# Keys and values of a decode attention kernel in tiles of four heads and 32 KB rows, where they were in tiles of two heads and 16 KB rows

## The chip, the cores and the metric

The kernel runs on one core of one Trainium2 chip. Its metric is the time on the device in microseconds (us), the median of several executions; lower is better. "Span" is the time from the first to the last instruction that the profiler saw in one execution; it is 1.7 to 2.1 us shorter than the time of the same execution. All runs compared here were in the fast state; e1 and e2, single looks below, have no state of their own (unknown), and lie within 0.3% of the fast runs beside them.

## The reference, cut to what matters

One token goes through an attention with 32 heads over a window of 4096 cached keys and values, times a gate from a small feed-forward block.

```python
# Hq = Hkv = 32 heads, Dh = 128, W = 4096 (the end of a cache of 32768), D = 512
q = (xn @ wq).reshape(B, 1, Hq, Dh).transpose(0, 2, 1, 3)
k = k_cache[:, :, Sk - W:, :]
v = v_cache[:, :, Sk - W:, :]
scores = einsum("bhqd,bhkd->bhqk", q, k) * Dh ** -0.5
o = einsum("bhqk,bhkd->bhqd", softmax(scores), v)
s = o.transpose(0, 2, 1, 3).reshape(B, 1, Hq * Dh) @ wo
# [the feed-forward block that gives g is cut: its weights are 4 % of the bytes]
return x + s * silu(g)
```

All is bfloat16. Keys and values are 67.1 MB of the 78.84 MB that the kernel reads, and each byte is used once.

## The kernel before

A step takes the keys of two heads. Each head fills every other partition, so a partition's row is 64 keys of 128 numbers, 16 KB in one piece of memory. VectorE computes a part of the scores itself (`k_vector`: a multiplication and a sum, two pieces to a step). TensorE turns the rest of the keys, ScalarE copies them out, and TensorE multiplies them with the query (`k_turn`, `k_scores`). The softmax goes by groups of four heads, so two steps; the values follow three steps behind the keys. All loads go through one queue, in the program's order.

```python
G, LAG, K_BUFS, V_BUFS = 4, 3, 6, 3
def load_kv(pool, cache, i, cuts=None):              # two heads, 2 MB
    t = pool.tile([P, CP, Dh], BF16, tag="kv", name="kv")          # CP = 64
    src = cache[0, 2 * i:2 * i + 2, W0:, :].rearrange("a (b c) d -> b a (c d)", b=P // 2)
    ...
def k_vector(s, kn, half):
    ...
    nc.vector.tensor_tensor(out=prod[:, 0:m, :], in0=kn[:, rows, :],
                            in1=q_bc[:, s:s + 1, :].to_broadcast([P, m, Dh]), op=ALU.mult)
    nc.vector.tensor_reduce(out=st[s // 2]["S"][:, s % 2, rows], in_=prod[:, 0:m, :], axis=AX.X, op=ALU.add)
...
for s in range(NP + LAG):                            # NP = 16 steps
    h = s - LAG
    kn = load_kv(k_pool, A_k_cache, s) if s < NP else None
    ...
    elif h >= 0:
        v = load_kv(v_pool, A_v_cache, h)
    ...
        k_vector(s, kn, 0)
        k_turn(s, kn)
        for g in turn:
            sm_turn(g)                               # maximum over partitions: PE, then DVE
        if s % 2 == 1 and s >= 3:
            sm_den((s - 3) // 2)                     # PE: sum over partitions
            sm_rden((s - 3) // 2)                    # DVE: 1 / sum
        k_scores(s)
        ...                                          # own scores, exponentials
        k_vector(s, kn, 1)
        if h >= 0:
            v_pair(h, v)                             # PE: values times weights
        ...
        if s % 2 == 1:
            sm_max(s // 2)                           # DVE: maximum along the row
```

Of the kernel before, what the change touches and what calls it, by code (L numbers as in the profile page):

```python
# [8 lines left out]
P = 128  # L9
BF16 = mybir.dt.bfloat16  # L10
# [9 lines left out]
LAG = 3  # L20
K_BUFS = 6
NE = 4
V_BUFS = 3
EARLY = 4
LATE = 14
# [4 lines left out]
def kernel(  # L30
# [24 lines left out]
    CP = 2 * W // P  # L55
# [7 lines left out]
    kt_pool = ctx.enter_context(tc.tile_pool(name="kt", bufs=2))  # L63
# [9 lines left out]
    small.tile([P, 64], BF16, name="pad")  # L73
# [22 lines left out]
    def load_kv(pool, cache, i, cuts=None):  # L96
        t = pool.tile([P, CP, Dh], BF16, tag="kv", name="kv")
        src = cache[0, 2 * i:2 * i + 2, W0:, :].rearrange("a (b c) d -> b a (c d)", b=P // 2)
        dst = t[:].rearrange("p c d -> p (c d)")
        cuts = cuts or (0, CP)  # L100
        for c0, c1 in zip(cuts, cuts[1:]):
            load(dst[:, c0 * Dh:c1 * Dh], src[:, :, c0 * Dh:c1 * Dh])
            if len(cuts) > 2 and c1 == cuts[-2]:
                load_rows(H - 4, 2)
        return t
# [13 lines left out]
    sel = wts.tile([H, H // 2, P // 2, 2], BF16, name="sel")  # L119
    nc.vector.tensor_copy(out=sel[:], in_=ident_bf[0:H, 0:H].rearrange("k (i a) -> k i a", a=2).unsqueeze(2)  # L120
                          .to_broadcast([H, H // 2, P // 2, 2]))
# [125 lines left out]
    q_bc = small.tile([P, H // 2, Dh], BF16, name="q_bc")  # L247
    for i in range(0, H // 2, 4):
        qb_ps = ps_tr.tile([P, 4, Dh], FP32, tag="pt", name="qb_ps")
        for k in range(4):  # L250
            nc.tensor.matmul(qb_ps[:, k, :], lhsT=sel[:, i + k, :, :].rearrange("k b a -> k (b a)"),
                             rhs=q_rows[:], start=True, stop=True)
        nc.scalar.copy(out=q_bc[:, i:i + 4, :], in_=qb_ps[:])
# [7 lines left out]
    for c in range(2):  # L261
# [14 lines left out]
    par = const.tile([P, 2], FP32, name="par")  # L276
    nc.vector.tensor_reduce(out=par[:], in_=ident_f[:].rearrange("p (b a) -> p a b", a=2), axis=AX.X,
                            op=ALU.max)
    two = const.tile([4, 1], FP32, name="two")
    nc.vector.tensor_reduce(out=two[:], in_=ident_f[0:4, 0:2], axis=AX.X, op=ALU.max)  # L280
    par_t = const.tile([4, P // 2, 2], FP32, name="par_t")
    nc.vector.tensor_scalar(out=par_t[:], in0=ident_f[0:4, 2:4].unsqueeze(1).to_broadcast([4, P // 2, 2]),
                            scalar1=two[:], scalar2=None, op0=ALU.add)
    md = const.tile([4, 2, 2], FP32, name="md")
    nc.vector.tensor_scalar(out=md[:], in0=ident_f[0:4, 2:4].unsqueeze(1).to_broadcast([4, 2, 2]),
                            scalar1=-1.0, scalar2=1e30, op0=ALU.add, op1=ALU.mult)




    pick_f = const.tile([P, 4, 2, 2], FP32, name="pick_f")
    for r in range(2):
        nc.vector.tensor_copy(out=pick_f[:, :, r, :],
                              in_=ident_bf[:, 32 * r:32 * r + 8].rearrange("p (i a) -> p i a", a=2))
# [3 lines left out]
    def nd(s):  # L298

        return 32 if s < EARLY else 40 if s < LATE else 32  # L300

    def k_open(s):
        if s % 2 == 0:
            st[s // 2] = {
                "sT": ps_s.tile([P, 2, CP - 32, 2], FP32, tag="sT", name="sT"),
                "S": sm_pool.tile([P, 2, CP], FP32, tag="S", name="S"),
            }

    def k_vector(s, kn, half):
        m = nd(s) // 2  # L310
        rows = slice(m * half, m * half + m)
        prod = prod_pool.tile([P, 20, Dh], BF16, tag="prod", name="prod")
        nc.vector.tensor_tensor(out=prod[:, 0:m, :], in0=kn[:, rows, :],  # L313
                                in1=q_bc[:, s:s + 1, :].to_broadcast([P, m, Dh]), op=ALU.mult)
        nc.vector.tensor_reduce(out=st[s // 2]["S"][:, s % 2, rows], in_=prod[:, 0:m, :], axis=AX.X,  # L315
                                op=ALU.add)
# [3 lines left out]
    def k_turn(s, kn):  # L320
        n = nd(s)
        kts[s] = kt_pool.tile([P, CP - 32, P], BF16, tag="kt", name="kt")
        w = 8 if n % 8 == 0 else 7
        assert (CP - n) % w == 0
        for b in range(0, CP - n, w):
            pt = ps_tr.tile([P, 8, P], BF16, tag="pt", name="pt")
            for i in range(w):
                nc.tensor.transpose(pt[:, i, :], kn[:, n + b + i, :], ident_bf[:])  # L328
            nc.scalar.copy(out=kts[s][:, b:b + w, :], in_=pt[:, 0:w, :])  # L329

    def k_scores(s):
        kt = kts.pop(s)
        for c in range(CP - nd(s)):
            nc.tensor.matmul(st[s // 2]["sT"][:, s % 2, c, :], lhsT=kt[:, c, :],  # L334
                             rhs=qT_bf[:, 2 * s:2 * s + 2], start=True, stop=True)


    def sm_own(g):
        s = st[g]
        n = nd(2 * g)  # L340
        own = sm_pool.tile([P, 2, CP - 32], FP32, tag="own", bufs=1, name="own")
        nc.scalar.mul(own[:, :, 0:CP - n], s["sT"][:, :, 0:CP - n, 1], par[:, 1:2])
        s["own"] = own

    def sm_max(g):
        s = st[g]
        n = nd(2 * g)
        own = s["own"]
        nc.vector.scalar_tensor_tensor(out=s["S"][:, :, n:CP], in0=s["sT"][:, :, 0:CP - n, 0],
                                       scalar=par[:, 0:1], in1=own[:, :, 0:CP - n],  # L350
                                       op0=ALU.mult, op1=ALU.add)
        s["m1"] = sm_pool.tile([P, 2], FP32, tag="m1", name="m1")
        nc.vector.tensor_reduce(out=s["m1"][:], in_=s["S"][:], axis=AX.X, op=ALU.max)  # L353

    def sm_turn(g):

        s = st[g]
        mt_ps = ps_misc.tile([2, P], FP32, tag="misc", name="mt_ps")
        nc.tensor.transpose(mt_ps[:], s["m1"][:], ident_f[:])
        mx = sm_pool.tile([2, 2], FP32, tag="mx", name="mx")  # L360
        nc.vector.tensor_reduce(out=mx[:], in_=mt_ps[:].rearrange("r (b a) -> r a b", a=2), axis=AX.X,
                                op=ALU.max)
        nc.vector.scalar_tensor_tensor(out=md[0:2],  # L363
                                       in0=ident_f[0:2, 0:2].unsqueeze(2).to_broadcast([2, 2, 2]),
                                       scalar=-scale, in1=mx[:].unsqueeze(1).to_broadcast([2, 2, 2]),
                                       op0=ALU.mult, op1=ALU.mult)

    def sm_exp(g):
        s = st[g]
        mb_ps = ps_misc.tile([P, G], FP32, tag="misc", name="mb_ps")  # L370
        nc.tensor.matmul(mb_ps[:], lhsT=par_t[:].rearrange("k b a -> k (b a)"),  # L371
                         rhs=md[:].rearrange("k r a -> k (r a)"), start=True, stop=True)
        mb = sm_pool.tile([P, G], FP32, tag="mb", name="mb")
        nc.scalar.copy(out=mb[:], in_=mb_ps[:])  # L374
        s["pT"] = sm_pool.tile([P, 2, CP, 2], BF16, tag="pT", name="pT")
        s["sum"] = sm_pool.tile([P, G], FP32, tag="sum", name="sum")
        for i in range(G):
            nc.scalar.activation(out=s["pT"][:, i // 2, :, i % 2], in_=s["S"][:, i // 2, :], func=ACT.Exp,  # L378
                                 scale=scale, bias=mb[:, i:i + 1], accum_out=s["sum"][:, i:i + 1])

    def sm_den(g):
        s = st[g]
        s["den"] = den_ps = ps_misc.tile([P, G], FP32, tag="misc", name="den_ps")
        nc.tensor.matmul(den_ps[:], lhsT=ones_f[:], rhs=s["sum"][:], start=True, stop=True)

    def sm_rden(g):
        s = st[g]
        den_ps = s["den"]
        s["rden"] = sm_pool.tile([P, G], FP32, tag="rden", name="rden")
        nc.vector.reciprocal(out=s["rden"][:], in_=den_ps[:])  # L390
# [11 lines left out]
    def load_wo(i):  # L402
        h0, n = blocks[i]
        t = k_pool.tile([P, 16, D], BF16, tag="kv", name="wo_16")
        wo_blk[i] = t[:, 0:n, :]
# [16 lines left out]
    def v_pair(h, v, c0=0, c1=CP):  # L422
        g, r = divmod(h, 2)
        s = st[g]
        if g in MOVED:
            if r == 0:
                s["ov"] = ps_o.tile([P, 4, Dh], FP32, tag="oT", name="ov")
                nc.tensor.matmul(s["ov"][:], lhsT=zero_bf[:], rhs=v[:, 0:4, :], start=True, stop=False,
                                 skip_group_check=True)
            for c in range(0, CP, 4):  # L430
                nc.tensor.matmul(s["ov"][32 * r:32 * r + 8],  # L431
                                 lhsT=s["pT"][:, r, c:c + 4, :].rearrange("p i a -> p (i a)"),
                                 rhs=v[:, c:c + 4, :], start=False, stop=c == CP - 4,
                                 skip_group_check=True)
            if r == 1:
                s["ov_sb"] = sm_pool.tile([P, 4, Dh], FP32, tag="ov_sb", bufs=1, name="ov_sb")
                nc.scalar.copy(out=s["ov_sb"][:], in_=s["ov"][:])
        else:
            if r == 0:
                s["oT"] = ps_o.tile([P, G], FP32, tag="oT", name="oT")  # L440
            for c in range(c0, c1):
                nc.tensor.matmul(s["oT"][:, 2 * r:2 * r + 2], lhsT=v[:, c, :], rhs=s["pT"][:, r, c, :],  # L442
                                 start=(c == 0), stop=(c == CP - 1))

    def v_add(g):
        s = st[g]
        s["oT"] = ps_misc.tile([P, G], FP32, tag="misc", name="oT")
        for j in range(4):
            nc.tensor.matmul(s["oT"][:], lhsT=s["ov_sb"][:, j, :],  # L449
                             rhs=pick_f[:, j, :, :].rearrange("p r a -> p (r a)"),  # L450
                             start=(j == 0), stop=(j == 3))

    def v_out(h, n):
# [192 lines left out]
```

## Time and profile before

| before | |
|---|---|
| time, median of 3 (lowest, highest) | 195.67 us (195.56, 195.85) |
| span of the profiled execution (another one, of 196.92 us) | 195.1 us |
| key load, 2 MB: issue to landing, median | 29.9 us |
| VectorE busy, share of the span | 74% |
| share of the DMA engines taken by the load queue | 96.1% |

Two lines of the page that the prediction does not show, from its groups of instructions (busy us, mean ns of one, idle time before):

```profile
L378 ACT ACTIVATE pT<-S,mb 128x64 bf16<-128x64 f32 x32 | 10.9, 356 | 0.2
...
L462 DVE TENSOR_TENSOR o<-oT,rden 128x2 bf16<-128x2 f32 x3 | 0.5, 160 | 11.1 <-PE oT L442 11.1
```

The first is the exponential over 64 columns, which has 128 after the change. The second shows VectorE's waits in the last part of the span: 11.1 us of idle time before three tiny instructions there, all for a product of TensorE.

### The profile page before, as it was taken

How to read it: one execution, taken by the hardware profiler on the slowest of the kernel's cores; microseconds unless marked ns; L12 is line 12 of the kernel's file. 1: busy time of each engine (PE TensorE's matmuls, PEld its weight loads, DVE VectorE, ACT ScalarE, POOL GpSimd, SP SyncE). 2: the span in 40 equal slices, each digit the busy share in tenths (PEclk: the TensorE clock that was granted, in tenths of full speed). 3: DMA queues.
4: the chain of work that ended last, by engine and by line, in shares of the span. 5: the costliest groups of instructions: out<-in, count | busy, mean ns of one | idle time of the engine just before them, and what ended most of it. 6: DMA issues, size and time to landing. Idle time of an engine off the chain costs nothing.

```text
span 195.1 us, 4727 instructions
## 1 busy us (share of the span) xinstructions
PE 137.3 (70%) x2108; PEld 105.2 (54%) x2108; DVE 145.2 (74%) x164; ACT 79.0 (40%) x173; POOL 6.3 (3%) x13
## 2 busy tenths in 40 slices
PE   0549779673785899397977957367767897957751
PEld 0434469563784945235967342167656536945640
DVE  0550109999999999999999999079899996982001
ACT  2003019881945742327467053152555018933000
POOL 2110007000000000000000000000000000000000
PEclk9999966967558559759687696965555569675555
DMA  6999999999999999999999999999999999999980
GB/s 200 413 415 410 373 427 423 428 420 430 430 423 430 430 425 427 433 430 430 423 430 430 427 433 427 430 433 430 430 430 427 430 422 432 423 433 420 402 311 4
DMA packets 7052, 79.13 MB, mean 406 GB/s; under 512 B 889, under 2 KB 1753, under 8 KB 2265
## 3 DMA queue, kind: packets, MB, share of 16 engines
q1 hardware_dynamic: 6880, 78.84, 96.1%
q8 instruction: 16, 0.26, 0.5%
q10 hardware_dynamic: 152, 0.00, 0.0%
q14 instruction: 4, 0.02, 0.0%
HBM read 78.84 MB, written 0.00 MB: 404 GB/s over the span
## 4 chain that ended last, share of the span: by engine, by line
DVE 47%; DMA 24%; PE 17%; ACT 5%; issue 4%; SPq 1%; POOL 1%; POOLq 0%
DVE S L315 28%; DVE prod L313 15%; DMA kv<-in_A_v_cache_dram 15%; DMA wo_rows<-in_A_wo_dram 7%; ACT kt L329 4%; PE yr_ps L507 3%; PE oT L442 3%; PE ov L431 3%; DMA x_bf<-in_A_x_dram 2%; PE qT_ps L239 2%; PE hr_ps L223 2%; SPq L78 1%; PE a_ps L212 1%; PE hr_ps L220 1%; DVE m L353 1%
## 5 line engine op out<-in xcount | busy, mean ns | idle before, releaser
L315 DVE TENSOR_REDUCE S<-prod 128x20 f32<-128x2560 bf16 (+1 forms) x32 | 83.8, 2620 | 1.1
L329 ACT COPY kt<-pt 128x1024 bf16<-128x1024 bf16 x54 | 50.9, 1021 | 28.0 <-PE pt L328 28.0
L313 DVE TENSOR_TENSOR prod<-kv,q_bc 128x2560 bf16<-128x2560 bf16 (+1 forms) x32 | 44.3, 1385 | 9.0 <-DMA kv<-in_A_k_cache_dram 6.4
L328 PE MATMUL pt<-ident_bf,kv 128*128 128x128 bf16 x432 | 41.0, 277 | 10.4 <-DMA kv<-in_A_k_cache_dram 8.8
L328 PEld LDWEIGHTS <-kv 128*128 128x128 bf16 x432 | 37.4, 129 | 13.7 <-DMA kv<-in_A_k_cache_dram 10.2
L334 PE MATMUL sT<-qT_bf,kt 128*128 128x2 bf16 x432 | 17.7, 165 | 11.8 <-ACT kt L329 11.2
L442 PE MATMUL oT<-pT,kv 128*128 128x2 bf16 x768 | 22.3, 165 | 4.6 <-DMA kv<-in_A_v_cache_dram 4.6
L442 PEld LDWEIGHTS <-kv 128*128 128x128 bf16 x768 | 21.4, 102 | 6.0 <-DMA kv<-in_A_v_cache_dram 5.9
L334 PEld LDWEIGHTS <-kt 128*128 128x128 bf16 x432 | 15.9, 102 | 14.8 <-ACT kt L329 14.0
L431 PE MATMUL ov<-kv,pT 128*8 128x512 bf16 x64 | 21.9, 517 | 0.0
L431 PEld LDWEIGHTS <-pT 128*8 128x8 bf16 x64 | 6.7, 109 | 13.9 <-issue 11.4
L378 ACT ACTIVATE pT<-S,mb 128x64 bf16<-128x64 f32 x32 | 10.9, 356 | 0.2
L371 PE MATMUL mb_ps<-md,par_t 4*128 4x4 f32 x16 | 3.9, 314 | 9.5 <-DVE md L363 9.5
L374 ACT COPY mb<-mb_ps 128x4 f32<-128x4 f32 x8 | 1.3, 162 | 19.3 <-PE mb_ps L371 19.3
L371 PEld LDWEIGHTS mb_ps<-md,par_t 4*128 4x128 f32 x16 | 3.4, 263 | 10.1 <-issue 8.8
L462 DVE TENSOR_TENSOR o<-oT,rden 128x2 bf16<-128x2 f32 x3 | 0.5, 160 | 11.1 <-PE oT L442 11.1
L466 ACT ACTIVATE o<-oT,rden 128x1 bf16<-128x1 f32 x26 | 4.7, 264 | 6.6 <-PE oT L449 4.7
L226 DVE COPY hr<-hr_ps 1x512 f32<-1x512 f32 x1 | 0.7, 677 | 7.9 <-PE hr_ps L223 7.9
L507 PE MATMUL yr_ps<-wo,ox 128*1 128x512 bf16 x16 | 6.3, 576 | 0.0
L378 ACT ACTIVATION_READ_ACCUMULATOR pT<-S,mb 128x1 f32 x32 | 6.0, 187 | 0.0
L157 PE MATMUL ln_ps<-x_f,ones_f 128*128 128x4 f32 x4 | 1.2, 364 | 6.1 <-DVE x_f L180 5.1
L215 ACT ACTIVATE a_bf<-a_ps 128x10 bf16<-128x10 f32 x1 | 0.2, 180 | 12.4 <-PE a_ps L212 12.4
(116 smaller groups left out, 95.1 us busy)
## 6 DMA issues: line engine op xcount, KB each, us to landing
kv<-in_A_k_cache_dram SPq DMA_DIRECT2D x16, 2048.0 KB, 29.9
kv<-in_A_v_cache_dram SPq DMA_DIRECT2D x15, 2048.0 KB, 26.9
wq_sb<-in_A_wq_dram SPq DMA_DIRECT2D x1, 4096.0 KB, 19.1
wo<-in_A_wo_dram SPq DMA_DIRECT2D x1, 2048.0 KB, 28.2
w_sb<-in_B_w_dram SPq DMA_DIRECT2D x1, 1376.0 KB, 6.7
w_sb<-in_B_w_dram SPq DMA_DIRECT2D x1, 1024.0 KB
wo<-in_A_wo_dram SPq DMA_DIRECT2D x1, 1024.0 KB, 26.8
kv<-in_A_v_cache_dram SPq DMA_DIRECT2D x1, 1024.0 KB
```

Of the source, the lines that this page charges most:

```text
L223: nc.tensor.matmul(hr_ps[:], lhsT=a_bf[0:m, i:i + 1], rhs=w4_sb[0:m, i, :], start=False, stop=(i == len(chunks) - 1))
L313: nc.vector.tensor_tensor(out=prod[:, 0:m, :], in0=kn[:, rows, :], in1=q_bc[:, s:s + 1, :].to_broadcast([P, m, Dh]), op=ALU.mult)
L315: nc.vector.tensor_reduce(out=st[s // 2]["S"][:, s % 2, rows], in_=prod[:, 0:m, :], axis=AX.X, op=ALU.add)
L328: nc.tensor.transpose(pt[:, i, :], kn[:, n + b + i, :], ident_bf[:])
L329: nc.scalar.copy(out=kts[s][:, b:b + w, :], in_=pt[:, 0:w, :])
L334: nc.tensor.matmul(st[s // 2]["sT"][:, s % 2, c, :], lhsT=kt[:, c, :], rhs=qT_bf[:, 2 * s:2 * s + 2], start=True, stop=True)
L371: nc.tensor.matmul(mb_ps[:], lhsT=par_t[:].rearrange("k b a -> k (b a)"), rhs=md[:].rearrange("k r a -> k (r a)"), start=True, stop=True)
L378: nc.scalar.activation(out=s["pT"][:, i // 2, :, i % 2], in_=s["S"][:, i // 2, :], func=ACT.Exp, scale=scale, bias=mb[:, i:i + 1], accum_o ...
L431: nc.tensor.matmul(s["ov"][32 * r:32 * r + 8], lhsT=s["pT"][:, r, c:c + 4, :].rearrange("p i a -> p (i a)"), rhs=v[:, c:c + 4, :], start=F ...
L442: nc.tensor.matmul(s["oT"][:, 2 * r:2 * r + 2], lhsT=v[:, c, :], rhs=s["pT"][:, r, c, :], start=(c == 0), stop=(c == CP - 1))
L466: nc.scalar.mul(o_blk[b][:, c + k:c + k + 1], st[g]["oT"][:, hl + k:hl + k + 1], st[g]["rden"][:, hl + k:hl + k + 1])
L507: nc.tensor.matmul(yr_ps[:], lhsT=ox_blk[i][:, t:t + 1], rhs=wo_blk[i][:, t, :], start=(t == 0), stop=(t == n - 1))
```

## The change

Its intent is to have fewer and larger transfers: a tile takes four heads, interleaved over the partitions, so a row is 32 KB and a load 4 MB. The group of the softmax becomes the group of a tile, which makes some of the mask work simpler. The key buffers hold as many bytes as before in half as many pieces (3 of 32 KB to a partition, where it was 6 of 16); the value buffers hold a third more in fewer pieces (2 of 32 KB, where it was 3 of 16). Cut to its core:

```diff
-LAG = 3
-K_BUFS = 6
+LAG = 2
+K_BUFS = 3
-V_BUFS = 3
+V_BUFS = 2
-    CP = 2 * W // P
+    CP = G * W // P                                   # 128 columns of 128 numbers
-    def load_kv(pool, cache, i, cuts=None):
-        src = cache[0, 2 * i:2 * i + 2, W0:, :].rearrange("a (b c) d -> b a (c d)", b=P // 2)
+    def load_kv(pool, cache, g, cuts=(0, CP)):
+        src = cache[0, G * g:G * g + G, W0:, :].rearrange("a (b c) d -> b a (c d)", b=PB)
 [... masks, own scores, softmax and output: from two heads to four ...]
-            for c in range(c0, c1):                   # 64 products of 2 columns, twice
+            for c in range(c0, c1):                   # 128 products of 4 columns in one go
+                nc.tensor.matmul(s["oT"][:], lhsT=v[:, c, :], rhs=s["pT"][:, c, :], ...)
 [... the step's order, now a step of four heads ...]
+            k_vector(s, kn, 0)
+            k_turn(s, kn, 0)
+            k_turn(s, kn, 1)
+            k_scores(s, 0)
+            if s > 0:
+                sm_turn(s - 1)
+                k_turn(s, kn, 2)
+                k_scores(s, 1)
+                sm_exp(s - 1)
+            if h - 1 in MOVED:
+                v_add(h - 1)
+                v_out(h - 1)
+            if s == 6:
+                ox_spread(0)
+            k_vector(s, kn, 1)
+            for b in range(3 if s > 0 else 2, nb):
+                k_turn(s, kn, b)
+                k_scores(s, b - 1)
+            k_scores(s, nb - 1)
+            sm_own(s)
 [...]
+            k_vector(s, kn, 2)
+            if s > 0:
+                sm_den(s - 1)
+                sm_rden(s - 1)
+            k_vector(s, kn, 3)
+            if h >= 0:
+                v_part(h, v)
+            sm_max(s)
```

## The prediction

> **What bounds the kernel now.** I began with the page's slices over time, because a kernel that reads 78.84 MB in 195.1 us may be limited by its transfers whatever the engines' shares say.
>
> ```profile
> span 195.1 us, 4727 instructions
> PE 137.3 (70%) x2108; PEld 105.2 (54%) x2108; DVE 145.2 (74%) x164; ACT 79.0 (40%) x173; POOL 6.3 (3%) x13
> DVE  0550109999999999999999999079899996982001
> DMA  6999999999999999999999999999999999999980
> GB/s 200 413 415 410 373 427 423 428 420 430 430 423 430 430 425 427 433 430 430 423 430 430 427 433 427 430 433 430 430 430 427 430 422 432 423 433 420 402 311 4
> q1 hardware_dynamic: 6880, 78.84, 96.1%
> ```
>
> The DMA row is 9 from the second slice to slice 38 of 40. No slice there is short of bytes for want of a request: the 16 engines always have something queued. VectorE is also at 9 for most of that time, so I then asked which of the two is the pacer. The chain of waits names VectorE first:
>
> ```profile
> DVE 47%; DMA 24%; PE 17%; ACT 5%; issue 4%; SPq 1%; POOL 1%; POOLq 0%
> DVE S L315 28%; DVE prod L313 15%; DMA kv<-in_A_v_cache_dram 15%; DMA wo_rows<-in_A_wo_dram 7%; ACT kt L329 4%; PE yr_ps L507 3%; PE oT L442 3%; PE ov L431 3%; DMA x_bf<-in_A_x_dram 2%; PE qT_ps L239 2%; PE hr_ps L223 2%; SPq L78 1%; PE a_ps L212 1%; PE hr_ps L220 1%; DVE m L353 1%
> ```
>
> I do not take that as the bound. The chain steps from the last bytes back to the work that freed a buffer and let a load be issued. But a key load takes a median of 29.9 us from issue to landing, and its own 2 MB need only about 4.9 us, so it stood behind other loads for 25 us. Making VectorE faster would lengthen that queue and bring the last byte no earlier. VectorE's timeline gives the same verdict:
>
> ```profile
> 68.03 1.49 DVE L313 TENSOR_TENSOR prod<-kv,q_bc 128x2560 bf16<-128x2560 bf16 x1
> 69.56 2.82 DVE L315 TENSOR_REDUCE S<-prod 128x20 f32<-128x2560 bf16 x1
> ...
> 86.16 1.49 DVE L313 TENSOR_TENSOR prod<-kv,q_bc 128x2560 bf16<-128x2560 bf16 x1
> ```
>
> From 68.03 to 86.16 it does the multiplications and sums of four heads: 18.1 us. The keys and values of four heads are 8.39 MB, at 429 GB/s 19.6 us. VectorE has 1.5 us to spare per four heads. **The bound is the rate of the DMA engines.**
>
> The remaining question is what sets that rate. I cut the DMA view to a stretch that holds only key and value rows (50 to 60 us) and one that holds only the weight wq (11.5 to 20.5 us), because wq is the one tensor that already comes at 32 KB to a partition (4096 KB over 128). First the keys and values:
>
> ```profile
> GB/s 374 655 374 374 468 562 187 374 655 374 374 468 562 187 374 655 374 374 468 562 187 374 749 281 281 468 655 94 374 655 374 281 468 655 94 374 749 374 281 468
> DMA packets 294, 4.29 MB, mean 429 GB/s; under 512 B 32, under 2 KB 32, under 8 KB 32
> q1 hardware_dynamic: 293, 4.28, 100.2%
> ```
>
> Then wq:
>
> ```profile
> GB/s 0 437 874 874 146 0 0 437 874 874 146 0 0 437 874 874 146 0 0 437 874 874 146 0 0 437 874 874 146 0 0 437 874 874 146 0 0 437 728 1019
> q1 hardware_dynamic: 111, 3.64, 104.8%
> ```
>
> The third number of a queue line is the time that packets took as a share of 16 engines times the window. Keys and values: 100.2% of 16 x 10 us is 160.3 us; 32 of the 293 packets are the tiny ones under 512 B, so 261 rows of 16 KB took **0.614 us** each. wq: 3.64 MB in 111 packets is 32.8 KB each, so a row goes as one packet; 104.8% of 16 x 9 us is 150.9 us, over 111 **1.360 us** each. Two 16 KB rows take 1.228. One 32 KB row takes 0.132 us more than the same bytes in two rows: 10.8%. The wq line also shows its shape: bytes are counted where a packet starts, and the starts come in bunches exactly six slices of 0.225 us apart, all engines in step at 1.35 us. In the trace's own packet records 90% of the 128 wq packets lie within 1.359 to 1.367 us, and the first 16 KB rows right behind them are at 0.611. So 16 x 32,768 B / 1.360 us = 386 GB/s, against 16 x 16,384 / 0.614 = 427. That is why slices 2 to 5 of the page, which wq fills in large part, show 410 to 373 and every slice of keys and values about 428.
>
> **What the Trainium skill says.**
> - "SBUF — State Buffer", section "The DMA setup-cost knee", tells authors to "coalesce into the largest single transfer you can". That speaks for the change, with gains from fixed cost. This trace shows no such cost left to save: with loads queued behind one another, 2 MB ones already move at 429 GB/s, and 4 MB wq moves slower.
> - "DMA: Bandwidth & Descriptors", section "Where 436 GB/s comes from", puts the ceiling at 435.2 GB/s. The trace agrees from below: 429. Even if the new form reached the ceiling, 63 MB would gain only about 2 us (estimate: 62.9/427 less 62.9/435).
> - The same page, section "Why a DMA increments its semaphore by 16 and not by 1", says that the number of engines is the largest k up to 16 that divides the slowest dimension of both sides. After the change these are 32 (source) and 128, so still 16 engines; 386 GB/s for wq, with 128 rows, needs all 16 as well.
> - The same page, section "Latency and other measured facts", tells of slower copies when rows lie a large power of two apart (some loss from 512 KiB on). That is the rival reason for wq's slowness, taken up below.
> No page I read gives a rate that falls as a row grows.
>
> **The change part by part.**
> 1. Loads. 32 key and value loads of 2 MB become 15 of 4 MB in whole rows of 32 KB, and the last value tile cut in rows of 16, 10, 4 and 2 KB. A whole load is 128 rows over 16 engines, 8 rows each: 8 x 1.360 = 10.88 us against 2 x 8 x 0.614 = 9.82. Fifteen times 1.06 is **+15.8 us**. The cut tile keeps short rows: no change. The wo loads keep 16 and 8 KB. Fifteen to sixteen fewer completion packets at 0.009 us per engine are 0.1 us, left out. All of this lies on the path, since the queue is never empty.
> 2. VectorE. The big pairs are the same forms and counts: 20 x (1.484 + 2.820) and 12 x (1.220 + 2.286) us. The 8 combining steps of 0.27 us become sums over 192 or 256 numbers; the nearest row, a sum over 256 numbers, took 0.581, so +0.3 x 8 = 2.4 us. Per four heads 18.4 us, against a new DMA time of 21.8: hidden.
> 3. ScalarE. 32 exponentials over 128 columns in place of 64: 0.356 plus about 0.06 each (a 1024-column copy takes 1.02, so some 1 ns a column), +2 us in all. Own-score copies 8 to 32 at about 0.3: +7. Query casts 4 to 2 at 0.6: -1.2. From 79 to about 87 us of a longer span: hidden.
> 4. TensorE. 432 turns, 432 scores, 768 + 64 value matmuls, all kept; scores and values have 4 columns for 2, which at 0.165 us of fill each is nothing. Hidden.
> 5. Buffers. Keys 6 x 16 KB become 3 x 32, values 3 x 16 become 2 x 32 per partition. A coarser buffer comes free later, so I walked the queue with 10.9 us per tile and 14 to 18.5 us of VectorE per group. First keys land at about 32 us rather than 26. The fourth key load issues at about 48 with work queued to 65; later loads come 15 to 20 us ahead of an empty queue; the narrowest is the last value tile, which waits for tile 6's forerunner to be consumed at about 184 with work to 192. The queue should not run dry.
> 6. Tail. After the last bytes, 16 small output matmuls in place of 8 (8 took 0.41): **+0.3 us**.
> Sum: 195.67 + 15.8 + 0.3 = 211.8; I say 211.5, for a little drift between engines at the end that may overlap.
>
> **The rivals.**
> - *A neutral outcome.* wq is slow for another reason (its engines read 256 KB apart, since each has 8 rows of 32 KB; the new loads' engines are 64 KB apart, 2 rows in each of 4 heads) or because of the early time. Then rows stay near 427 GB/s and the time is 195 to 197. Against it: the time is constant to a nanosecond or so, no jitter as I would expect of colliding streams; wo rows of 16 KB lie 128 KB apart between engines, and the slices that hold them show no dip; w3, loaded just before wq, ran at 435 GB/s between 4 and 7 us; the row right behind is fast. I give this 11%.
> - *A gain.* Larger rows save per-packet cost and some startup. The most it can make is the 2 us of the ceiling: 193.5. Over 2% faster needs 191.8, which I hardly believe: 2%.
> - *Starvation or VectorE as the bound on top of the slower rows.* If my walk is wrong by a buffer, a gap of 5 to 8 us opens somewhere: 217 or more. Slower transfers make this less likely, as they give VectorE 3 us per group. 5%.
>
> **Range and chances.** With the row time as measured, the sum's uncertainties (row time by 1%, tail and gaps by 2 us) give 207 to 215. That should hold 8 times in 10, nearly all the rest being the neutral case. Faster 0.02, same 0.11, slower 0.87.
>
> **What would show it.** Right: slices of keys and values at 384 to 390 GB/s with the DMA row still 9; about half the packets; VectorE waiting on key loads about 3 us per group, so its row falls from 9 to 7 or 8; the span longer by 15 to 17 us, spread evenly over the eight groups. Wrong in step 1: slices at 427 and a span near 195. Wrong in step 5: slices with 0 to 6 in the DMA row. Wrong in step 2 or 3: VectorE at 9 throughout beside a DMA row below 9.

## The result, and the profile after

| | before | after |
|---|---|---|
| time, median of 6 (lowest, highest) | 195.66 us (195.45, 195.85) | 201.69 us (201.47, 204.44) |
| ratio after to before, 95% interval | | 1.033 (1.028 to 1.038) |
| span of the profiled execution | 193.9 us (second profile, see below) | 199.9 us |

A ratio here is the mean time of one kernel's fast runs over that of the other's fast runs of the same rounds, so it is not quite the ratio of the medians. The changed kernel is slower by 6.0 us in the median. The prediction had said 211.5. All outputs are right.

The page of the changed kernel, the same rows that the prediction showed of before:

```profile
span 199.9 us, 4705 instructions
...
PE 134.0 (67%) x2098; PEld 103.6 (52%) x2098; DVE 145.8 (73%) x160; ACT 85.3 (43%) x193; POOL 6.0 (3%) x13
...
DVE  1640105999966999999999999999659999691201
...
DMA  6999999999999999999999999999999999839850
GB/s 211 407 471 420 420 456 449 434 426 416 426 420 423 453 448 426 430 423 433 420 423 446 439 393 459 439 426 420 430 446 433 430 408 443 368 94 393 319 216 0
...
q1 hardware_dynamic: 4720, 78.84, 93.1%
```

The slices of the middle, 8 to 33, are at 430 GB/s on average (mean of the row), as before. The announced 384 to 390 is nowhere to be seen. The row that differs is the end: in slices 35 and 36 (170 to 180 us) the DMA row falls to 8 and 3, and the rate to 368 and 94. So the changed kernel is not slower per byte. It has a hole near the end, and an end that comes late after the hole.

The price of a row, by the method of the prediction: the DMA view of after from 50 to 60 us, only keys and values,

```profile
DMA packets 145, 4.23 MB, mean 423 GB/s; under 512 B 16, under 2 KB 16, under 8 KB 16
...
q1 hardware_dynamic: 145, 4.23, 97.9%
```

gives 97.9% of 160 us over 145 less 16 tiny packets: 156.6 / 129 = 1.214 us for a row of 32 KB, against 1.228 for two of 16 KB. In the trace's packet records the mean over all 1920 such rows is 1.217 us. The row costs less than its halves, not a tenth more.

Why then was wq at 1.360? The same view from 11.5 to 20.5 us, where only wq is in flight, first of a second profile of the unchanged kernel (e1 below), then of after:

```profile
q1 hardware_dynamic: 134, 3.85, 99.1%
```

```profile
q1 hardware_dynamic: 140, 4.13, 106.2%
```

In the prediction's profile each took 1.360 us. Here they are 134 less 11 tiny ones at 99.1% (1.16 by this coarse reading, since packets cross the window's ends; 1.213 in the packet records) and 140 less 14 at 106.2%, likewise 1.213. The same load of the same kernel took 1.36 us a row in one execution and 1.21 in the next. The first profile of before had a span of 195.1 us with slow wq rows, the second 193.9 with fast ones; 8 rows to an engine times 0.147 us are 1.2 us, which is the whole difference. Even where wq is slow its length is not the reason: in e3 below, wq's rows took 1.359 us, and the key rows of the same 32 KB right behind them 1.22. So from here on after (whose wq rows were fast) is compared with e1.

Now the six microseconds. VectorE's waits (for what: us in total, times, longest), from its first key product to its last row maximum. First before (e1):

```profile
DVE prod L313 <- DMA kv<-in_A_k_cache_dram: 7.0, 3, 4.6
DVE prod L313 <- ACT q_bc L253: 2.1, 1, 2.1
DVE mx L361 <- PE mt_ps L359: 0.8, 1, 0.8
```

then after:

```profile
DVE rden L368 <- PE den_ps L363: 5.4, 2, 3.4
DVE prod L303 <- DMA kv<-in_A_k_cache_dram: 5.1, 1, 5.1
DVE spread L443 <- ACT o L436: 3.4, 1, 3.4
```

Before, VectorE waited 7.0 us for keys while at work: it was ahead of the bytes, as the prediction had it. After, it waited for keys once, 5.1 us for the first 4 MB tile, and never again; its other 8.8 us are waits for TensorE and ScalarE. An engine that never waits for bytes after its start is no longer paced by them. The timelines (start, length) give the sum. The first product starts at 28.85 us in e1, and at 32.37 in after; the last row maximum ends at 174.13 and 178.91; the spans end at 193.9 and 199.9. So after loses 3.5 us at the start, 1.3 in the middle (146.54 less 145.28) and 1.2 at the end (20.99 less 19.77), 6.0 in all. The middle looks cheap only because e1's includes 7.0 us of waiting for bytes that VectorE could have used for a late start, and after's has none of that to give.

The waits in after's timeline, and after them, from the queue's own timeline, the issue of the last load of values:

```profile
32.37 1.23 DVE L303 TENSOR_TENSOR prod<-kv,q_bc 128x2048 bf16<-128x2048 bf16 x1 [5.05 <-DMA kv<-in_A_k_cache_dram]
...
61.59 0.18 DVE L368 RECIPROCAL rden<-den_ps 128x4 f32<-128x4 f32 x1 [3.42 <-PE den_ps L363]
...
147.00 0.43 DVE L443 TENSOR_TENSOR spread<-o,mt 128x256 bf16<-128x256 bf16 x1 [3.41 <-ACT o L436]
...
174.65 0.18 DVE L368 RECIPROCAL rden<-den_ps 128x4 f32<-128x4 f32 x1 [1.95 <-PE den_ps L363]
```

```profile
178.05 1.88 SPq L79 DMA_DIRECT2D kv<-in_A_v_cache_dram  x3
```

What is to be seen: the reciprocal of the softmax sum stands in VectorE's list between two of its four key pieces, and waits for a sum that TensorE reaches late in its own list (`sm_den`, `sm_rden` in the diff). `spread` waits for an output that goes through a block of 32 value products with 512 columns. And the load of the last values is issued at 178.05 us, since its buffer comes free only when TensorE has done all 128 products of an earlier tile, from 174.47 to 178.02: that is the hole in the slices.

Last, TensorE's own waits from 170 us to the end, the two largest lines of each, e1 first and then after:

```profile
PE oT L442 <- DMA kv<-in_A_v_cache_dram: 3.9, 4, 1.2
PE mt_ps L359 <- DVE m L353: 1.5, 1, 1.5
```

```profile
PE oT L413 <- issue: 1.8, 2, 0.9
PE sT L319 <- ACT kt L314: 1.0, 1, 1.0
```

Before, the tail's products wait for the bytes of the values. After, none does. Its two stops of 0.9 us are marked "issue", which means that nothing that the page shows was waited for. The full record of the trace says more. Number TensorE's instructions in order of time (matmuls, weight loads and the few entries of its sequencer): in the fourteen traces of this study TensorE stopped in this way for 0.4 us or more 37 times, every time at number 193 or 194 beyond a multiple of 256, and went on 1.2 to 1.6 us after the end of a packet of 16 KB in the queue "instruction" (after: packets ending at 185.53 and 191.98 us, work going on at 186.95 and 193.49). That the stops are waits for the next block of instructions is an inference, but a narrow one. e1 has no such stop in its tail, after has 1.8 us of them.

The tail is close to a tie all the same: in after the last values have landed at 193.4 us, and TensorE takes them up at 195.2.

### The profile page after: what moved, and what is told of

Same layout as the page of the kernel before. It is cut to its first block, busy times and chain, and to the rows that moved or that the text cites. A ratio compares the mean times of both kernels' runs of the same rounds, so it can differ in the third digit from the quotient of the medians.

```text
span 199.9 us, 4705 instructions
## 1 busy us (share of the span) xinstructions
PE 134.0 (67%) x2098; PEld 103.6 (52%) x2098; DVE 145.8 (73%) x160; ACT 85.3 (43%) x193; POOL 6.0 (3%) x13
## 4 chain that ended last, share of the span: by engine, by line
DVE 49%; PE 20%; DMA 16%; ACT 11%; issue 3%; ACTq 0%; DVEq 0%
DVE S L305 29%; DVE prod L303 15%; DMA kv<-in_A_k_cache_dram 14%; ACT kt L314 5%; PE ov L405 5%; ACT pT L357 4%; PE oT L413 4%; PE pt L312 4%; PE yr_ps L476 3%; PE sT L319 2%; DMA x_bf<-in_A_x_dram 2%; PE y_ps L152 1%; PE den_ps L363 1%; DVE S L333 1%; PE mb_ps L350 1%
## 5 line engine op out<-in xcount | busy, mean ns | idle before, releaser
L312 PE MATMUL pt<-ident_bf,kv 128*128 128x128 bf16 x432 | 48.3, 286 | 3.5 <-DMA kv<-in_A_k_cache_dram 2.4
L319 PE MATMUL sT<-qT_bf,kt 128*128 128x4 bf16 x432 | 20.4, 169 | 18.6 <-ACT kt L314 18.3
L413 PE MATMUL oT<-pT,kv 128*128 128x4 bf16 x768 | 21.5, 166 | 1.8 <-issue 1.8
L405 PE MATMUL ov<-kv,pT 128*16 128x512 bf16 x64 | 17.7, 447 | 0.0
L357 ACT ACTIVATE pT<-S,mb 128x128 bf16<-128x128 f32 x32 | 13.9, 568 | 0.2
L350 PE MATMUL mb_ps<-md,par_t 5*128 5x4 f32 x16 | 3.9, 311 | 13.2 <-DVE md L345 12.9
L405 PEld LDWEIGHTS <-pT 128*16 128x16 bf16 x64 | 6.4, 102 | 10.4 <-issue 5.1
L350 PEld LDWEIGHTS mb_ps<-md,par_t 5*128 5x128 f32 x16 | 3.4, 260 | 14.4 <-issue 12.5
L328 ACT ACTIVATE own<-sT,par 128x48 f32<-128x48 f32 (+1 forms) x32 | 7.6, 358 | 3.7 <-PE sT L319 3.7
L341 PE MATMUL mt_ps<-ident_f,m 128*1 128x128 f32 x8 | 2.7, 334 | 6.4 <-DVE m L335 6.4
## 6 DMA issues: line engine op xcount, KB each, us to landing
kv<-in_A_v_cache_dram SPq DMA_DIRECT2D x1, 1280.0 KB, 11.5
```

Source lines behind the costliest of these rows:

```text
L312: nc.tensor.transpose(pt[:, i, :], kn[:, nd(g) + 8 * b + i, :], ident_bf[:])
L319: nc.tensor.matmul(st[g]["sT"][:, 8 * b + i, :], lhsT=kt[:, i, :], rhs=qT_bf[:, G * g:G * g + G], start=True, stop=True)
L328: nc.scalar.mul(s["own"][:, 0:m, a], s["sT"][:, 0:m, a], par[:, a:a + 1])
L350: nc.tensor.matmul(mb_ps[:], lhsT=par_t[:].rearrange("k b a -> k (b a)"), rhs=md[:], start=True, stop=True)
L357: nc.scalar.activation(out=s["pT"][:, :, a], in_=s["S"][:], func=ACT.Exp, scale=scale, bias=mb[:, a:a + 1], accum_out=s["sum"][:, a:a + 1])
L405: nc.tensor.matmul(s["ov"][:], lhsT=s["pT"][:, c:c + 4, :].rearrange("p i a -> p (i a)"), rhs=v[:, c:c + 4, :], start=(c == 0), stop=(c == ...
```

## The experiments

The theories. *The dry queue*: the hole in the DMA row (the engines half idle from 174 us, empty from 177 to 179) holds up the last bytes, and the end with them. *The late chain*: the bytes no longer set the end; VectorE, ScalarE and TensorE form one chain in program order, which starts later with a 4 MB tile, stops for its own coarse pieces, and ends late; the hole is a symptom. *The row price*: rows of 32 KB do cost something, in some form. Where an expectation uses letters, A is the dry queue; the others are what the text itself says of them. The runs were made in four sets (e1 to e4, e5 to e8, e9 to e11, e12), each on one chip together with runs of before, whose medians were 195.6, 195.8, 195.7 and 195.7 us. After was not run again in them, so every gain over after is a difference to the 201.69 us of the first set. A rival that the traces answer is TensorE's granted clock (the page's PEclk as a mean): 0.716 in e1, 0.652 in after. But it was 0.599 in e9 and 0.609 in e12, whose profiled executions took 197.14 and 195.98 us, so a lower mean clock alone does not make the 6 us.

**e1. The kernel before, again.** No edit; one look.

> The kernel before, unchanged, profiled a second time: is the 1.36 us row of wq a lasting property of that kernel's load or an accident of one run? If the destination or the row size made it slow, wq rows take 1.36 us again (slices 3 to 5 near 390 to 410 GB/s). If the place of the weight in HBM in that one execution or that one chip made it slow, this run may show about 1.21 us. The span should be within 1.5 us of 195.1 either way.

Measured: 195.75 us, span 193.9, wq rows at 1.213 us. That is what settled that wq's 1.36 us was of that one execution.

**e2. Before, with wq at another place in the on-chip memory.** Is it the destination address?

```diff
+    wq_sb = wts.tile([P, KC, HD], BF16, name="wq_sb")
     w2_sb = wts.tile([P, KC, D], BF16, name="w2_sb")
 ...
-    wq_sb = wts.tile([P, KC, HD], BF16, name="wq_sb")
```

> The kernel before, with the tile of wq given out first, so that wq lies 26,368 bytes lower in each partition. If the destination address made its rows slow, they take 1.21 us here and 1.36 in the unchanged kernel of the same call; otherwise both runs agree. Span 194 to 196.

Measured: 196.03 us in one run, wq rows at 1.213. With e1 equal, this run says nothing on the address. Over all fourteen profiled executions the median row was at 1.213 us in ten and at 1.359 in three (before, e3, e10). In one, e7, the load changed over half way: of the eight rows of each engine, the second to fourth took 1.213 us and the last three 1.359. So it is one of two values, and not even fixed for one load. e1 to e4 ran on the same chip, e3 among them, so the chip alone does not decide it, nor does the kernel (before and e1 are the same). What does stays open.

**e3. After, with the value product that holds the last buffer moved ahead.** The load of the last values comes earlier.

```diff
             k_vector(s, kn, 1)
+            if s == NG - 1:
+                v_part(h, v)
             for b in range(3 if s > 0 else 2, nb):
 ...
-            if h >= 0:
+            if 0 <= h and s < NG - 1:
                 v_part(h, v)
```

> The changed kernel, with only the value product of group 5 moved ahead of the last key blocks of step 7, so that the last value load can be issued earlier. Theory A (the load that waits for a value buffer, and the dry queue after it, cost the time): the load issues near 170 instead of 178, the gap in the DMA row goes, the time falls by 3 to 5 us to about 197 to 198. Theory B (the chain of the key work, late from the start and held up in its steps, sets the end, and the dry queue is only a symptom): the gap goes, but the time stays within 1 us of 201.7, as the products after the last softmax still come one after another.

Measured: 203.14 us (201.83 to 204.8), ratio 1.038. The windows of 5 us (from:to, length, busy us of PE, PEld, DVE, ACT and POOL with their instructions, clock, DMA share, GB/s), first after:

```profile
175.00:180.00 5.00, 3.60 (x116) 3.04 (x112) 4.46 (x8) 0.93 (x6) 0.00 (x0) 0.50 0.30 85
...
190.00:195.00 5.00, 4.06 (x149) 3.57 (x138) 0.00 (x0) 0.00 (x0) 0.00 (x0) 0.50 0.57 206
```

then e3:

```profile
175.00:180.00 5.00, 3.88 (x56) 3.29 (x53) 0.53 (x2) 3.88 (x7) 0.00 (x0) 0.50 0.96 396
...
190.00:195.00 5.00, 3.62 (x122) 3.01 (x118) 1.04 (x5) 0.00 (x0) 0.00 (x0) 0.50 0.01 4
```

The hole is gone: 0.96 of the DMA engines from 175 to 180 us where it was 0.30, and from 190 us on there are hardly any bytes left. The last load landed at 190.2 us in place of 194.1. The end of this execution came at 203.0 in place of 199.9. (It was the slowest of the e3 runs and had slow wq rows, which is 1.2 us of the 3; the medians differ by 1.5.) Bytes that arrive 4 us earlier, and an end that is no earlier: in e3 the bytes do not set the end. The time lies outside both expectations (the second had within 1 us of 201.7), since the edit is not clean: the last row maximum went from 178.6 to 183.9 us, because VectorE's reciprocal now waited 4.5 us behind the product that had been moved ahead of its sum. So e3 does not show what closing the hole alone would bring. What speaks against the dry queue in after itself is TensorE's list above: from 170 us on it waits for no value bytes, in after as in e3.

**e4. After, with the first key tile in two loads of 2 MB.** The start as before, all else as after.

```diff
-        kn = load_kv(k_pool, A_k_cache, s) if s < NG else None
+        kn = load_kv(k_pool, A_k_cache, s, (0, 64, CP) if s == 0 else (0, CP)) if s < NG else None
```

(A condition in `load_kv` that recognizes the tail's cut tile by its number of cuts is adapted, here and in e8.)

> The changed kernel, with only the first key load cut in two loads of 2 MB. VectorE's first multiplication starts near 29 instead of 32.4. Theory B: the whole key chain moves up by 3 to 4 us and the time falls by 2.5 to 4. Theory A: the last value load also moves up with it, so this run alone does not tell them apart; together with the previous run it does. Theory C (the start does not matter, later waits absorb it): no change.

Measured: 200.79 us (199.89 to 201.59), ratio 1.026: 0.9 less in the median, with ranges that touch (after's lowest is 201.47), where I had expected 2.5 to 4. VectorE did start at 29.35 us, 3.0 earlier. But at the row maxima of the first four groups the lead was 2.2, after the first block of 512-column products 1.2, and at the last maximum (178.08 against 178.62) 0.5. The waits of VectorE show who took it:

```profile
DVE rden L368 <- PE den_ps L363: 5.3, 2, 3.4
DVE spread L443 <- ACT o L436: 3.4, 1, 3.4
DVE mx L343 <- PE mt_ps L341: 2.2, 3, 0.9
...
DVE S L333 <- ACT own L328: 0.7, 1, 0.7
```

The reciprocal and `spread` still wait their 8.7 us, and new waits have opened: up to the last maximum 1.8 us of `mx` (the maximum over partitions; the rest of the 2.2 comes later and is in after too) where TensorE had not got there yet, and 0.7 for ScalarE's own scores. Together they are the 2.5 us that the lead shrank by. A late start is one of several waits in a chain; taking one away lets the next one grow.

**e5. After, with VectorE's two long waits taken out of its way.** The reciprocal goes behind the fourth key piece, `spread` behind the second, so that their inputs are there.

```diff
+            k_vector(s, kn, 1)
             if s == 6:
                 ox_spread(0)
-            k_vector(s, kn, 1)
 ...
                 sm_den(s - 1)
-                sm_rden(s - 1)
+                if s == 6:
+                    sm_rden(s - 1)
             k_vector(s, kn, 3)
+            if s > 0 and s != 6:
+                sm_rden(s - 1)
```

> The changed kernel, with VectorE's two in-step waits moved to where their data is long ready: the reciprocal of the denominators behind the fourth key part (but not in step 6), the spread of block 0 behind the second part. It had sat 3.4, 3.4 and 2.0 us in them. If VectorE's chain sets the end (theory B with VectorE as the pacer), the time falls by 5 to 8 us to 194 to 197. If TensorE's in-order queue sets it (theory D: 9 us value products of groups 1 and 3 in one block, key turns and softmax behind them), VectorE only waits elsewhere and the time falls by less than 2 us.

Measured: 199.59 us (197.85 to 200.12), ratio 1.018; 2.1 us less than after, between the two expectations. The waits that the edit aimed at are gone, one has come in their place:

```profile
DVE prod L303 <- DMA kv<-in_A_k_cache_dram: 5.1, 1, 5.1
DVE pick L453 <- PE ox_ps L451: 2.6, 1, 2.6
```

In the profiled execution, the fastest of e5, the last maximum began at 173.0 us, 5.6 earlier than in after, and the end, 196.1, came only 3.8 earlier. Of what VectorE gained, the tail kept a third; its "issue" stops come to 2.0 us. The last value load also came 3.6 us earlier (174.46), so the hole shrank along with the chain.

**e6. After, without the blocks of 512-column products.** TensorE's two long blocks (9.15 us the second, 131.79 to 140.94) become 128 small products like those of the other groups.

```diff
-MOVED = (1, 3)
+MOVED = ()
```

> The changed kernel, with the value products of groups 1 and 3 done like all others (128 small products, 3.6 us) in place of 32 wide ones (9.1 us in one block). Theory D: the waits behind these blocks in steps 4 and 6 go, and the time falls by 2.5 to 4 us. VectorE as the pacer: under 1 us.

Measured: 199.33 us (198.96 to 200.38), ratio 1.019: 2.4 less than after, just short of the 2.5 to 4 expected. The last maximum came 1.7 us earlier.

**e7. After, with the seventh group's value product ahead of the last softmax.** TensorE would use the time in which the softmax of the last group waits for VectorE.

```diff
             ox_spread(1)
+            v_part(h, v)
             sm_turn(NG - 1)
+            v_out(h)
             ox_pick(1)
 ...
-            v_part(h, v)
-            v_out(h)
```

> The changed kernel, with the value product of group 6 ahead of the last group's softmax instead of behind it. Its values land at 177 and it waited until 183. If the end is a chain of compute after the last softmax (theory B or D), 3.6 us of it move away and the softmax comes some 2 us later: the time falls by 1.5 to 3.5 us. If the last bytes set the end (theory A), no change.

Measured: 203.49 us (203.3 to 204.22), ratio 1.040: 1.8 us more where 1.5 to 3.5 less had been expected. A miss. The product does not fill a gap there; the softmax stands behind it.

```profile
DVE mx L343 <- PE mt_ps L341: 4.8, 3, 3.6
```

```profile
195.40 2.08 PE L413 MATMUL oT<-pT,kv 128*128 128x4 bf16 x72 [2.83 <-issue]
```

The maximum over partitions waits up to 3.6 us for TensorE (first line: in total, times, longest), so all that follows of the last softmax is late, and one of the stops without a cause in the profile has grown to 2.83 us (second line, in TensorE's timeline). This stop is of the kind described above (instruction 194 beyond a multiple of 256, 1.2 us after a 16 KB packet); all of them after 170 us come to 3.2 us, in after to 1.8. The wq rows of this execution, 1.287 us in the mean, are another 0.6. These two make 2.0, and the two profiled executions differ by 1.9: on these two, the move itself is worth about nothing. Whether the stops and the slow rows were there in e7's other three runs, which were as slow, is not known.

**e8. After, with every whole tile in two loads of 16 KB rows.** Grain and order of the computation as after, rows and loads as before: the row price alone.

```diff
-            v = load_kv(v_pool, A_v_cache, h)
+            v = load_kv(v_pool, A_v_cache, h, (0, 64, CP))
 [the same for all key tiles]
```

> The changed kernel, with every whole key and value tile loaded by two DMAs in rows of 16 KB instead of one in rows of 32 KB (same buffers, same waits for them). Against the kernel that cuts only the first key tile (200.8) it tells the price of the row size alone. From the traces, two 16 KB rows take 1.228 us and one 32 KB row 1.217, so 15 tiles differ by 1.3 us of transfer, which a queue that is not the bound hides: 200 to 201.5. If the 1.36 us of my prediction were the price of a long row, this would be 10 us faster than the changed kernel.

Measured: 200.14 us (199.47 to 200.52), ratio 1.022. It contains the early start of e4, so it is to be held against e4's 200.79 (other rounds): 0.65 us less with the smaller rows, within the two ranges. The rate in the stretch from 40 to 160 us, e8 first, then e4 with its rows of 32 KB:

```profile
40.00:160.00 120.00, 83.18 (x1154) 62.58 (x1152) 110.35 (x84) 61.32 (x142) 0.00 (x0) 0.63 1.01 429
```

```profile
40.00:160.00 120.00, 84.64 (x1152) 63.44 (x1151) 109.12 (x84) 61.48 (x142) 0.00 (x0) 0.61 1.00 431
```

429 and 431 GB/s: the row's length is worth half a per cent, in favour of the long row, and the kernel has no use for it.

**e9. After, with e4, e5 and e6 together.** Do the three cures add up?

> The changed kernel with three cures at once: first key tile in two loads, VectorE's in-step waits moved, value products of groups 1 and 3 done like the others. Alone they gave 0.9, 2.1 and 2.4 us. If each was bounded by the others (one in-order chain over three engines), together they give more than their sum of 5.4: the last group's maximum near 169 instead of 178.6, the last value load issued near 171 with no dry slice, the end set by the last bytes again: 194.5 to 196. If they simply add: 196 to 197.5. If they overlap: 198 to 199.

Measured: 196.92 us (196.45 to 198.18), ratio 1.007. That is 4.8 less than after; the single gains are 0.9, 2.1 and 2.4, in sum 5.4. VectorE now waits 1.9 us for a key tile in the middle: the bytes begin to set the pace again.

**e10. e9, with the sixth group's product cut into slices of 16 columns between the last key blocks.**

```diff
                 k_scores(s, b - 1)
+                if s == NG - 1:
+                    v_part(h, v, 16 * b - 48, 16 * b - 32)
 ...
-                v_part(h, v)
+                v_part(h, v, 16 * nb - 48 if s == NG - 1 else 0)
```

> The previous kernel, with the value product of group 5 spread in slices of 16 columns between the key blocks of step 7, so that its buffer comes free earlier. If the last value load still comes late there, 0.5 to 1.5 us better than the previous one; if the queue is never dry there any more, no change or up to 1 us worse, as the slices delay the last keys.

Measured: 196.9 us (196.71 to 197.88), ratio 1.006, no change. The slices did not bring the load forward: it was issued at 175.17 us against 174.85 in e9. The profile fell on the slowest of the e10 runs, with slow wq rows (1.2 us); allowing for those, the load came about a microsecond earlier than in e9 at most. So this run adds nothing on the dry queue.

**e11. Before, with the first two key loads swapped.** VectorE cannot start until both are there. If before is bound by its bytes, that costs nothing.

```diff
+    k1 = load_kv(k_pool, A_k_cache, 1)
     for s in range(NP + LAG):
 ...
-        kn = load_kv(k_pool, A_k_cache, s) if s < NP else None
+        kn = k1 if s == 1 else load_kv(k_pool, A_k_cache, s) if s < NP else None
```

> The kernel before, with its first two key loads in the other order, so that the first tile that the engines need lands some 4.9 us later, as in the changed kernel (VectorE starts near 32 instead of 29.4). If the kernel before has slack because its end is set by the bytes, no change: within 0.5 us of 195.7. If its VectorE chain were the bound, 2.5 to 3 us slower.

Measured: 195.66 us (195.58 to 195.88), ratio 1.000 (0.999 to 1.002).

```profile
32.36 1.22 DVE L313 TENSOR_TENSOR prod<-kv,q_bc 128x2048 bf16<-128x2048 bf16 x1 [4.77 <-DMA kv<-in_A_k_cache_dram]
```

This is the cleanest pair. VectorE starts at 32.36 us, within a hundredth of where after starts, 3.5 later than in e1, and the time is the same as ever: before has the slack. In after the same lateness is part of the 6 us.

**e12. e9, with a load of wo later and the last values' first 64 columns ahead of the small products of the tail.** A try at a version that beats before.

```diff
             wo_blk[0], wo_blk[1] = wo_24[:, 0:16, :], wo_24[:, 16:24, :]
+        if h == 4:
             load_wo(0)
 ...
+            v_part(h, v, 0, cuts[1])
             ox_pick(few_block)
 ...
-            for c0, c1 in zip(cuts, cuts[1:]):
+            for c0, c1 in zip(cuts[1:], cuts[2:]):
```

> The kernel of the three cures (196.9), with two more: the wo load of block 0 queued behind the seventh key tile instead of ahead of it (VectorE had waited 1.9 us for that tile at 135.7), and the first 64 value columns of the last group computed before the small chain that finishes the rows of the group before it, where TensorE sat idle for about 1.5 us. If the compute chain still sets the end, about 1.5 to 3 us less: 194 to 195.4, ahead of both kernels. If the end is already set by the bytes in it, no more than 0.5 us less.

Measured: 196.13 us (195.94 to 197.9), ratio 1.003 (0.999 to 1.007): 0.8 less than e9, between the two expectations, and the same as before: 5.6 of the 6.0 us recovered, with rows of 32 KB in all whole tiles but the first. TensorE's waits from 170 us on say why it stops there:

```profile
PE oT L413 <- DMA kv<-in_A_v_cache_dram: 2.5, 2, 1.9
...
PE y_ps L152 <- issue: 0.9, 1, 0.9
```

It waits for the bytes of the values again, as before did: both kernels are then at the rate of the DMA engines. e12's last bytes landed at 188.65 us, 0.6 before e1's (189.29), and yet its span is 0.3 longer (194.2): after the bytes comes the stop of 0.9 us in the second line. No version here beats before.

## Why the prediction was right or wrong

- **The bound of before** (the DMA engines, with VectorE 1.5 us to spare per four heads): right. e11 delays VectorE by 3.5 us and the time does not move. One reading beside it was loose: wq begins at 10.5 us, so slice 2 (413 GB/s) is not its doing, and slice 5, at 373, is at 389 in e1 too, where wq is fast.
- **Step 1, the loads, +15.8 us: this is the step that failed.** It took the row time of one load, in one execution, for the price of its row length. The evidence was of good quality but of one kind: 128 packets within a hundredth of a microsecond are one observation of a state, not 128. The rival (wq is slow for another reason) was named and given 11%, and the argument against it, that a constant time cannot be a disturbance, was the wrong one: the fast state is as constant. Measured: 1.217 us against 2 x 0.614; 15 tiles times 8 rows times about 0.011 us makes a gain of 1.3 us. A second profile of the kernel before would have shown it.
- **Step 2, VectorE, +2.4 us and hidden:** the eight sums took 0.34 to 0.41 us, and the busy total went from 145.3 (e1) to 145.8: +0.5. The size was too large; "hidden" was the second step that failed. It counted VectorE's busy time per group against the bytes' and left out what VectorE waits for inside a group: 8.8 us, and 5.1 for the first tile. The walk of step 5 even had the first keys at 32 us in place of 26, and put no price on it.
- **Step 3, ScalarE, about 87 us:** 85.3 measured. The exponential over 128 columns took 0.568 us and not 0.42; the copies of own scores came to 7.6 us busy in all, where 32 times 0.3 makes 9.6. The sum is near because the errors cancel.
- **Step 4, TensorE, hidden:** the busy time did not grow (136.0 in e1, 134.0 in after). Yet its order is on the path: e6, which only replaces its long blocks, gave 2.4 us.
- **Step 5, the buffers, no dry queue:** wrong, there is a hole from 174 to 179 us; the walk had the last value tile's load issue at about 184 and it was 178.05. But in after and in e3 TensorE waits for no value bytes at the end, so the hole is not what set it.
- **Step 6, the tail, +0.3 us:** 1.2 from the last row maximum to the end. What was left out is that the tail's small products no longer lie in the shade of arriving bytes, and that they meet 1.8 us of stops ("issue"), of which e1's tail has none.
- **The rivals:** the nearest was the third, starvation or VectorE as the bound, at 5%. It was tied to the slower rows and to 217 us; without them, its 5 to 8 us are the size that was measured, but they come from waits of VectorE, not from a buffer too few. The most that *a gain* could make was put at 2 us; its own figures give 2.7 (147.3 less 144.6). The signs that the prediction set itself answered clearly: slices at 427 refute step 1, a 3 in the DMA row refutes step 5, and a VectorE row mostly at 9 beside a DMA row that ends below 9 is close to the sign set for steps 2 and 3.

So the direction was right by luck: the step that was to make the kernel slower did not, and steps called hidden did. Shown: bytes cost no more, a late start plus in-order waits of coarse pieces put the chain of VectorE, ScalarE and TensorE behind the bytes (e5, e6, e4 by a little, and all three in e9), and with these undone the time is that of before (e12). The same cures brought the last value load forward (178.05 us in after, 174.85 in e9, 171.66 in e12), so how soon the dry queue would have become the next limit was not tested apart. Open: what decides wq's row time in an execution; how much of the 6 us the "issue" stops make, as no run takes them out; and how the last 0.8 us of e9 split between the two edits of e12, which ran only together.

## What to carry to other kernels

Where a kernel is bound by its bytes and its queue is never empty, larger transfers had next to nothing to gain here (431 against 429 GB/s), and they coarsen everything that hangs on a tile: the first start, the return of a buffer, the pieces between which an in-order engine can look after other work. Count for such a change not only busy time per group against bytes per group, but the waits inside a group, in program order on each engine. And before a price is taken from one load of one execution, profile the same kernel a second time.

## What the Trainium skill lacked or had wrong

- "DMA: Bandwidth & Descriptors" does not say that the row time of one and the same load can take one of two values: 32 KB rows of wq took 1.213 us in ten of fourteen executions and 1.359 in three, and changed from the one to the other within the load in one (e7). It was no matter of the chip or kernel alone. The prediction fell over this.
- The same page, section "Where 436 GB/s comes from", says that between HBM and SBUF the HBM side binds, at about 358 GB/s. Here, with one core at work, loads from HBM ran at 429 to 431 GB/s for 120 us (e8, e4), so it did not bind at that figure. The same paragraph calls a measured 425 GB/s near the rate of the fabric; what its sentence leaves out is the condition for 358 (both cores of a pair loading), which the page has elsewhere.
- "SBUF — State Buffer", section "The DMA setup-cost knee", advises to coalesce into the largest transfer one can. With loads queued behind one another, 2 MB loads in 16 KB rows moved 429 GB/s and 4 MB loads in 32 KB rows 431; the coarser tiles cost 6.0 us by their grain. The page lacks the condition that the fixed cost must be exposed.
- "Runtime: NRT & Kernel Launch", section "Instruction fetch mechanics", calls the cost of crossing a 16 KiB block of 256 instructions "mostly hidden". By count the traces agree: TensorE's list has 16 or 17 such crossings in each, and one to five of the crossings show a stop of 0.4 us or more (none in e1's tail). But the 37 stops all lie at such crossings, and those that show are long: 0.9 and 0.9 us in the tail of after, 2.83 in e7. The page gives no size for one that is not hidden. That they are waits for instructions is inferred from their place and from the packets, not shown by a run that removes them.
